# VectorE's two half steps of a pair declared independent of each other, with an empty instruction between direct neighbours

## The chip, the cores and the metric

The kernel runs on one core of one Trainium2 chip. The metric is the device time of one execution in microseconds (us). Engines are named as in the profile: PE is TensorE, PEld its weight loads, DVE is VectorE, ACT is ScalarE, POOL is GpSimd, SP is SyncE.

## The reference

For each of four batches of 6080 tokens with 256 channels a channel attention is computed, and its output goes, token by token, through a feed-forward layer with a rational function in the middle:

```python
def _attn_ref(q, k, v, tau):                     # q, k, v: (4, 6080, 256)
    qn = q / (np.linalg.norm(q, axis=1, keepdims=True) + 1e-06)
    kn = k / (np.linalg.norm(k, axis=1, keepdims=True) + 1e-06)
    s = kn.transpose(0, 2, 1) @ qn / tau
    a = softmax of s over its last axis           # 256 x 256 for each batch
    return v @ a

def _moe_ref(x, w_in, w_out, a, b):              # x: (24320, 256), w_in: (256, 2048), w_out: (2048, 256)
    h = x @ w_in
    h2 = h * h
    h3 = h2 * h
    P = a[0] + a[1] * h + a[2] * h2 + a[3] * h3
    Q = 1.0 + np.abs(b[0]) * np.abs(h) + np.abs(b[1]) * h2
    g = P / (Q + 1e-06)
    return g @ w_out
```

## The kernel before

**Tiling.** The 24320 tokens are cut into 48 groups of 512 (the last of each batch has 448). The 2048 columns of the hidden layer are cut into 8 pairs of two blocks of 128. `pair(m, ...)` is one such pair for one group, so there are 384 of them. The softmax matrix of a batch is multiplied into `w_in` once for each batch (`fuse`), so a pair needs only one product of the values `vhi`, `vlo` with the fused weights `w`.

**A pair on its engines.** The product lands in `hx`, a PSUM tile of two banks, one bank for each block of the pair (tags `hA` and `hB`, index x = 0 and 1 below). There are three such tiles, named hx_176 to hx_178 in listings. PE fills each bank with six matmuls (`mm1`). Then ACT computes `uu` and `d` from hx, and from d the reciprocal `r` (two more steps); DVE turns hx into the numerator ("num", hx<-uu,fast,hx, both banks at once), then writes the high part of the quotient ("quot", gh<-hx,fast,r). What is left is done bank by bank in `tail(x)`: POOL multiplies the denominator by gh ("again", d<-d,gh), DVE subtracts that from the numerator ("rest", hx<-hx,fast,d) and multiplies by r ("last", gl<-hx,r), which is the low part. PE adds gh and gl times `w_out` into `acc` (`out_hi`, `out_lo`). "last" of a bank is the last reader of that bank of hx: after it, PE may fill the bank for a later pair.

**The order.** All steps are put into a list with planned costs and due times (`LAG`, `TIME`), and `Planner.order()` turns it into one fixed program order for each engine. The engine objects are wrapped by `InOrder`, which keeps each engine's instructions in that order. What an instruction waits for is not written by hand: the framework finds dependencies by tile, and it sees the two banks of one hx tile as one tile. `apart` tells it that two instructions on different banks of one hx tile don't depend on each other, but before the change only when they run on different engines (`other is not eng`). So on DVE, "rest" of x = 1 waits for whatever DVE did last on bank 0 of the same tile, and "last" of x = 0 waits for the last step on bank 1 if that stands ahead of it. An instruction can hold a limited number of waits itself; others stand ahead of it on the engine's queue as instructions that only wait (EVENT_SEMAPHORE in the profile).

The kernel has a quick and a general body and picks one at run time by the coefficients. The quick body is the one that runs here. Nearly all instructions are recorded at line 79, since `InOrder` issues them all; tiles tell them apart.

Of the kernel before, what the change touches and what calls it, by code (L numbers as in the profile page):

```python
# [125 lines left out]
def flat(bufs):  # L126
    return [x for b in bufs for x in (b.both if isinstance(b, Pair) else [b])]
# [165 lines left out]
def tile_channel_attention_rational_ffn(  # L293
# [36 lines left out]
    FRONT = 10  # L330

    half = [None]
    seen = {}

    def apart(eng, ins):


        if half[0] is None:
            return
        slot, bank, rest = half[0]  # L340
        for other, old, used in seen.get((slot, 1 - bank), ()):
            if other is not eng and not used & rest:
                tc.declare_no_dep(ins.ins, old.ins, reason="the two use different banks of one tile")
        mine = seen.setdefault((slot, bank), [])
        mine.append((eng, ins, rest))
        del mine[:-40]

    pe = InOrder(tc, nc.tensor, apart)
    dve = InOrder(tc, nc.vector, apart)
    act = InOrder(tc, nc.scalar, apart)  # L350
    pool = InOrder(tc, nc.gpsimd)
    sp = InOrder(tc, nc.sync)
# [15 lines left out]
    def buf(tag, shape, dtype=F32, name=None):  # L368


        def view(slot):
            sizes = dict(zip("abc", shape[1:]))
            t = homes[tag][slot]
            if t.dtype != dtype:
                t = t.bitcast(dtype)
            t = t[:, : math.prod(shape[1:])]
            names = " ".join(sizes)
            return t.rearrange(f"p ({names}) -> p {names}", **sizes) if len(sizes) > 1 else t

        homes.setdefault(tag, 0)  # L380
        homes[tag] = max(homes[tag], math.prod(shape[1:]))
        return Buf(tag, view)
# [75 lines left out]
    def body(quick):  # L458
        lag, when = (LAG, TIME) if quick else (GENERAL_LAG, GENERAL_TIME)
        plan = planner(when)  # L460
        II, T0 = when["pair"], when["start"]
        def step(eng, cost, key, fn, reads=(), writes=(), port=False, rank=None):
            new = [b for b in flat(writes) if b.tag is not None and not b.writers]
            used = {id(b): b for b in (*flat(reads), *flat(writes))}.values()
            own = [b for b in used if b.tag in ("hA", "hB")]
            rest = [b for b in used if b.tag not in ("hA", "hB")]

            def run():
                for b in new:
                    b.tile = b.view(b.slot)  # L470
                at = {(b.slot, b.tag == "hB") for b in own}
                if len(at) == 1:
                    half[0] = *at.pop(), {(b.tag, b.slot) if b.tag else id(b) for b in rest}
                fn()
                half[0] = None

            plan.add(eng, cost, key, run, reads, writes, port, rank)
# [4 lines left out]
        def piece(side, m, at, c):  # L482
# [71 lines left out]
            else:  # L554
                dst, ok = None, w_out_ok[m]
                where = slice(2 * m, 2 * m + 2)
                whi, wlo = (x[:, where].rearrange("p f e -> p (f e)") for x in (w_out_hi, w_out_lo))
            step("SP", 1.45, at, load, (), [raw])
            step("ACT", 0.67, c, rescale, [raw], [kept])
            one, two = (0.45, 0.7) if port else (0.62, 0.7)  # L560
            step("DVE", one, c, low_bits, [kept], [work], port)
            step("DVE", two, c + 0.1, high_bits, [kept, work], [work], port)
            step("DVE", one, c + 0.2, power, [work], [work], port)
# [278 lines left out]
        def pair(m, at, vparts, w, acc):  # L842
# [3 lines left out]
            s = n / 512  # L846
            (vhi, vlo), (whi, wlo) = vparts, w
            hx = banks()
            d, r = buf("d", [P, 2, GT]), buf("r", [P, 2, GT])
            y = buf("uu", [P, 2, GT], F32, "uu")  # L850

            def c(b):
                return b[:, :, :n]

            def due(name):
                x = lag[name]
                return at + (x[p] if isinstance(x, tuple) else x)

            def mm1(i):
                idx = 0  # L860
                for e in range(NC2):
                    for a, x in ((whi, vhi), (whi, vlo), (wlo, vhi)):
                        pe.matmul(
                            hx[:, i, :n], a[:, e, i * P : (i + 1) * P], x[:, e, :n],
                            start=(idx == 0), stop=(idx == 3 * NC2 - 1),
                        )
                        idx += 1

            for i in range(2):
                fn = lambda i=i: mm1(i)  # L870
# [8 lines left out]
                                start=(first and i == parts[0] and a is w[0]), stop=(last and i == 1 and a is w[-1]),  # L879
                            )  # L880

            def put(eng, per, fixed, name, fn, reads, writes, rank=None, later=0.0):
                step(eng, per * s + fixed, due(name) + later, fn, reads, writes, False, None if rank is None else at + rank)

            if quick:
                fn = lambda: act.activation(c(d), c(hx), AF.Abs)
                put("ACT", 0.87, 0.16, "abs", fn, [hx], [d], 1.0)
                fn = lambda: act.activation(c(y), c(hx), AF.Square, bias=half2)
                put("ACT", 0.87, 0.25, "zz", fn, [hx], [y], 1.0)
                fn = lambda: act.activation(c(d), c(d), AF.Square, bias=half1)  # L890
                put("ACT", 0.87, 0.22, "shift", fn, [d], [d])
                fn = lambda: dve.scalar_tensor_tensor(c(hx), c(y), kappa, c(hx), op0=ALU.add, op1=ALU.mult)
                put("DVE", 1.06, 0.23, "num", fn, [y, hx], [hx])
                fn = lambda: act.activation(c(r), c(d), AF.Abs_reciprocal_sqrt, bias=eps)
                put("ACT", 0.87, 0.22, "root", fn, [d], [r], 6.0)
                fn = lambda: pool.tensor_scalar(c(d), c(d), ones[:, 0:1], eps, op0=ALU.mult, op1=ALU.add)
                put("POOL", 1.06, 0.1, "one", fn, [d], [d])
                first = c0
            else:
                kk = buf("uu", [P, 2, GT], F32, "kk")  # L900
                fn = lambda: act.activation(c(kk), c(hx), AF.Abs, scale=b1)
                put("ACT", 0.87, 0.25, "kk", fn, [hx], [kk], 1.0)
                fn = lambda: dve.scalar_tensor_tensor(c(d), c(kk), b0, c(hx), op0=ALU.add, op1=ALU.mult)
                put("DVE", 1.06, 0.22, "prod", fn, [kk, hx], [d], 1.0)
                fn = lambda: act.activation(c(d), c(d), AF.Abs)
                put("ACT", 0.87, 0.2, "absd", fn, [d], [d])
                fn = lambda: act.activation(c(y), c(hx), AF.Identity, scale=a3, bias=a2)
                put("ACT", 0.87, 0.33, "slope", fn, [hx], [y], 1.0)
                fn = lambda: dve.tensor_tensor(c(y), c(y), c(hx), op=ALU.mult)
                put("DVE", 1.06, 0.16, "num1", fn, [y, hx], [y])  # L910
                fn = lambda: dve.scalar_tensor_tensor(c(hx), c(y), a1, c(hx), op0=ALU.add, op1=ALU.mult)
                put("DVE", 1.06, 0.23, "num2", fn, [y, hx], [hx])
                fn = lambda: act.activation(c(r), c(d), AF.Abs_reciprocal_sqrt, bias=ONE)
                put("ACT", 0.87, 0.2, "root", fn, [d], [r], 6.0)
                fn = lambda: pool.tensor_scalar(c(d), c(d), ones[:, 0:1], ONE, op0=ALU.mult, op1=ALU.add)
                put("POOL", 1.06, 0.07, "one", fn, [d], [d])
                first = a0
            fn = lambda: act.activation(c(r), c(r), AF.Square)
# [3 lines left out]
            ghi, glo = buf("gh", [P, 2, GT], F32R), buf("gl", [P, 2, GT], F32R)  # L922
            ghi_ok = Buf()
            t_ok, glo_ok = ([Buf() for _ in range(2)] for _ in range(2))
            fn = lambda: dve.scalar_tensor_tensor(c(ghi), c(hx), first, c(r), op0=ALU.add, op1=ALU.mult)
# [11 lines left out]
            def tail(x):  # L937
                h = hx.both[x]
                fn = lambda: pool.tensor_tensor(d[:, x, :n], d[:, x, :n], ghi[:, x, :n].bitcast(F32), op=ALU.mult)
                put("POOL", 1.16, 0.1, "again", fn, [d, ghi, ghi_ok], [t_ok[x]], later=0.1 * x)  # L940
                fn = lambda: dve.scalar_tensor_tensor(
                    hx[:, x, :n], hx[:, x, :n], first, d[:, x, :n], op0=ALU.add, op1=ALU.subtract
                )
                put("DVE", 0.53, 0.22, "rest", fn, [h, d, t_ok[x]], [h], later=0.1 * x)
                fn = lambda: dve.tensor_tensor(glo[:, x, :n], hx[:, x, :n], r[:, x, :n], op=ALU.mult)
                put("DVE", 0.53, 0.14, "last", fn, [h, r, *([glo] if x else [])], [glo_ok[x], *([] if x else [glo])], 10.0, 0.1 * x)

            for x in range(2):
                tail(x)
                out_hi(x)  # L950
                out_lo(x)
# [70 lines left out]
        for G in range(TG):  # L1022
            b, g = divmod(G, NG)
            at = T0 + G * NFP * II
# [57 lines left out]
```

## Time and profile before

| | |
|---|---|
| median of 3 runs | 2476.43 us (2476.23 to 2478.35) |
| the profiled execution, its own time | 2477.43 us |
| its span, first to last instruction | 2475.4 us |
| busy share of the span | PE 96%, DVE 89%, ACT 88%, POOL 72% |
| mean granted TensorE clock | 0.987 |

The profiled execution is 1.0 us above the median, and 2.0 us of its time lie outside the span. Busy shares are averages over parts of the run that differ: the first 200 us load weights and compute the first attention; in three later parts the attention of the next batch is mixed in between pairs; and in between the pairs run with little else.

### The profile page before, as it was taken

What the parts mean: (1) busy time and instruction counts of PE and PEld (TensorE: products, weight loads), DVE (VectorE), ACT (ScalarE), POOL (GpSimd) and SP (SyncE); (2) the same over time, 40 slices, a digit from 0 to 9 for tenths busy, and PEclk for the clock granted to TensorE, in tenths of its full rate; (3) what the DMA queues carried; (4) which work ended last, traced back from release to release, by engine and by line L of the source; (5) the groups of instructions that cost most, each with busy time, mean ns of one, the idle gap of its engine ahead of it and who ended that gap; (6) DMA issues with size and microseconds to landing.
All of it is one profiled execution on the core that took longest, in us unless ns stands there. A gap on an engine that the chain in (4) does not pass through costs nothing.

```text
span 2475.4 us, 30913 instructions
## 1 busy us (share of the span) xinstructions
PE 2375.3 (96%) x10400; PEld 1942.0 (78%) x10400; DVE 2196.5 (89%) x2684; ACT 2169.3 (88%) x2156; POOL 1770.5 (72%) x1353
## 2 busy tenths in 40 slices
PE   5799999999999999999999999999999999999997
PEld 4677777888788877778788888777878777777786
DVE  6879999988978899999987889999997999999996
ACT  3589999978877899999977789999997999999996
POOL 4387777787679877777768986777774777767765
PEclk9799999999999999999999999999999999999999
DMA  8542112252267611211236731112111110100100
GB/s 248 138 113 42 28 18 35 47 131 56 41 147 171 116 24 18 35 18 18 34 69 157 163 58 25 27 18 35 17 18 20 30 19 18 35 18 18 33 9 18
DMA packets 416890, 141.19 MB, mean 57 GB/s; under 512 B 351344, under 2 KB 406064, under 8 KB 416720
## 3 DMA queue, kind: packets, MB, share of 16 engines
q1 hardware_dynamic: 408176, 108.04, 20.2%
q0 software_dynamic: 8544, 31.07, 7.1%
q8 instruction: 84, 1.38, 0.2%
q14 instruction: 86, 0.70, 0.1%
HBM read 83.10 MB, written 24.90 MB: 44 GB/s over the span
## 4 chain that ended last, share of the span: by engine, by line
PE 74%; DVE 12%; issue 5%; ACT 3%; POOL 2%; DMA 2%; SPq 1%; DVEq 0%; POOLq 0%; ACTq 0%
PE hx L79 40%; PE acc L79 34%; DVE hx L79 5%; DVE gl L79 4%; DVE gh L79 2%; POOL d L79 1%; SPq L79 1%; ACT d L79 1%; ACT r L79 1%; DMA kq<-in_q_dram 1%; DVE orow L79 1%; ACT uu L79 1%; DMA d<-in_moe_w_in_dram 1%; ACT L79 0%; DMA r<-in_k_dram 0%
## 5 line engine op out<-in xcount | busy, mean ns | idle before, releaser
L79 POOL TENSOR_TENSOR d<-d,gh 128x512 f32<-128x512 f32 (+1 forms) x768 | 977.9, 1304 | 498.0 <-DVE gh L79 495.2
L79 PE MATMUL hx<-vhi,w 128*128 128x512 f32 (+1 forms) x3072 | 1046.1, 395 | 30.0 <-DVE gl L79 27.6
L79 PEld LDWEIGHTS hx<-vhi,w 128*128 128x128 f32 x3072 | 579.8, 189 | 195.0 <-DVE gl L79 77.0
L79 DVE SCALAR_TENSOR_TENSOR hx<-hx,fast,d 128x512 f32<-128x512 f32 (+1 forms) x768 | 574.7, 748 | 82.3 <-POOL d L79 53.4
L79 PE MATMUL hx<-vlo,w 128*128 128x512 f32 (+1 forms) x1536 | 598.6, 390 | 0.0
L79 DVE TENSOR_TENSOR gl<-hx,r 128x512 fp32r<-128x512 f32 (+1 forms) x768 | 516.9, 681 | 40.3 <-PE acc L79 3.2
L79 POOL TENSOR_SCALAR d<-d,ones,fast 128x1024 f32<-128x1024 f32 (+1 forms) x384 | 470.7, 1226 | 101.0 <-ACT r L79 100.6
L79 ACT ACTIVATE uu<-hx,fast 128x1024 f32<-128x1024 f32 (+1 forms) x384 | 423.1, 1102 | 135.3 <-PE hx L79 122.9
L79 DVE SCALAR_TENSOR_TENSOR hx<-uu,fast,hx 128x1024 f32<-128x1024 f32 (+1 forms) x384 | 487.2, 1269 | 45.3 <-ACT d L79 35.6
L79 DVE SCALAR_TENSOR_TENSOR gh<-hx,fast,r 128x1024 fp32r<-128x1024 f32 (+1 forms) x384 | 485.8, 1265 | 42.1 <-ACT r L79 34.8
L79 PE MATMUL acc<-gh,w_out_hi 128*128 128x512 f32 (+1 forms) x1536 | 476.7, 392 | 3.2 <-DVE gh L79 2.4
L79 PE MATMUL acc<-gl,w_out_hi 128*128 128x512 f32 (+1 forms) x1536 | 473.8, 390 | 4.4 <-DVE gl L79 4.3
L79 PE MATMUL acc<-gh,w_out_lo 128*128 128x512 f32 (+1 forms) x1536 | 470.3, 387 | 0.0
L79 ACT ACTIVATE r<-d,fast 128x1024 f32<-128x1024 f32 (+1 forms) x384 | 439.7, 1145 | 10.9
L79 ACT ACTIVATE d<-d,fast 128x1024 f32<-128x1024 f32 (+1 forms) x384 | 439.4, 1145 | 8.5
L79 ACT ACTIVATE d<-hx 128x1024 f32<-128x1024 f32 (+1 forms) x384 | 386.5, 1007 | 38.2 <-PE hx L79 32.3
L79 ACT ACTIVATE r<-r 128x1024 f32<-128x1024 f32 (+1 forms) x384 | 403.7, 1052 | 9.1
L79 PEld LDWEIGHTS acc<-gh,w_out_hi 128*128 128x128 f32 x1536 | 287.6, 188 | 65.0 <-ACT orow L79 3.3
L79 PEld LDWEIGHTS acc<-gl,w_out_hi 128*128 128x128 f32 x1536 | 287.8, 188 | 62.9 <-DVE gl L79 6.4
L79 PEld LDWEIGHTS acc<-gh,w_out_lo 128*128 128x128 f32 x1536 | 288.6, 188 | 57.8
L79 PEld LDWEIGHTS hx<-vlo,w 128*128 128x128 f32 x1536 | 290.3, 189 | 52.4
L79 PE MATMUL hx<-kq 128*128 128x256 f32 (+1 forms) x592 | 136.7, 385 | 17.8 <-DVE r L79 17.8
(105 smaller groups left out, 1154.8 us busy)
## 6 DMA issues: line engine op xcount, KB each, us to landing
ssq<-sq POOLq DMA_DIRECT2D x54, 512.0 KB, 4.9
out_dram<-orow SPq DMA_DIRECT2D x178, 128.0 KB, 3.2
vst<-in_v_dram SPq DMA_DIRECT2D x176, 128.0 KB, 3.8
kq<-in_k_dram SPq DMA_DIRECT2D x78, 256.0 KB, 4.4
kq<-in_q_dram SPq DMA_DIRECT2D x78, 256.0 KB, 4.8
d<-in_moe_w_in_dram SPq DMA_DIRECT2D x8, 512.0 KB, 6.9
ssq<-sq POOLq DMA_DIRECT2D x6, 448.0 KB, 5.3
r<-in_k_dram SPq DMA_DIRECT2D x10, 256.0 KB, 6.2
```

The lines of the kernel that those rows point to most:

```text
L79: ins = op(*args, **kwargs)
```

## The change

`apart` gets a fourth entry, `lane`, which is (number of the pair, x) for the steps "rest" and "last" on DVE and None for all others. Two DVE instructions of the same pair and of different x are now declared independent as well. Where two such steps are direct neighbours in DVE's order, `run` issues `dve.nop()` between them, since the declaration would otherwise also remove the order between them.

```diff
     def apart(eng, ins):
         if half[0] is None:
             return
-        slot, bank, rest = half[0]
-        for other, old, used in seen.get((slot, 1 - bank), ()):
-            if other is not eng and not used & rest:
+        slot, bank, rest, lane = half[0]
+        for other, old, used, side in seen.get((slot, 1 - bank), ()):
+            beside = lane is not None and side is not None and lane[0] == side[0] and lane[1] != side[1]
+            if beside or (other is not eng and not used & rest):
                 tc.declare_no_dep(ins.ins, old.ins, reason="the two use different banks of one tile")
         mine = seen.setdefault((slot, bank), [])
-        mine.append((eng, ins, rest))
+        mine.append((eng, ins, rest, lane))
...
             def run():
                 for b in new:
                     b.tile = b.view(b.slot)
+                old = recent.get(eng)
+                if lane is not None and old is not None and old[0] == lane[0] and old[1] != lane[1]:
+                    dve.nop()
+                recent[eng] = lane
...
-                put("DVE", 0.53, 0.22, "rest", fn, [h, d, t_ok[x]], [h], later=0.1 * x)
+                put("DVE", 0.53, 0.22, "rest", fn, [h, d, t_ok[x]], [h], later=0.1 * x, lane=(m, x))
...
-                put("DVE", 0.53, 0.14, "last", fn, [h, r, *([glo] if x else [])], [glo_ok[x], *([] if x else [glo])], 10.0, 0.1 * x)
+                put("DVE", 0.53, 0.14, "last", fn, [h, r, *([glo] if x else [])], [glo_ok[x], *([] if x else [glo])], 10.0, 0.1 * x, (m, x))
```

No instruction changes its place: on all five engines the rows of the two built programs stand in the same order. What changes is what DVE's instructions wait for. Below is a piece of the difference on DVE, with waits shown, from the middle of the quick body (it runs at 1021.8 to 1031.4 us in the profiled execution before). DVE_49 is a wait for an earlier instruction of DVE itself, Pool_49, PE_49 and Activation_49 are waits for POOL, PE and ACT; a minus is the program before, a plus is the changed one, and x2 are two equal rows, one behind the other.

```order
 L79 SCALAR_TENSOR_TENSOR hx_177<-hx_177,fast,d_123 128x512 [waits Pool_49]
 L79 TENSOR_TENSOR gl_174<-hx_177,r_129 128x512 [waits DVE_49,PE_49]
-L79 SCALAR_TENSOR_TENSOR hx_177<-hx_177,fast,d_123 128x512 [waits DVE_49,Pool_49]
+L79 SCALAR_TENSOR_TENSOR hx_177<-hx_177,fast,d_123 128x512 [waits Pool_49]
 L79 SCALAR_TENSOR_TENSOR gh_173<-hx_176,fast,r_131 128x1024 [waits PE_49,Activation_49]
 L79 TENSOR_TENSOR gl_174<-hx_177,r_129 128x512 [waits DVE_49,PE_49]
 L79 SCALAR_TENSOR_TENSOR hx_178<-uu_127,fast,hx_178 128x1024 [waits PE_49,Activation_49]
-L79 SCALAR_TENSOR_TENSOR hx_176<-hx_176,fast,d_125 128x512 [waits Pool_49]
-L79 SCALAR_TENSOR_TENSOR hx_176<-hx_176,fast,d_125 128x512 [waits DVE_49,Pool_49]
-L79 TENSOR_TENSOR gl_175<-hx_176,r_131 128x512 [waits DVE_49,PE_49]
-L79 TENSOR_TENSOR gl_175<-hx_176,r_131 128x512 [waits PE_49]
+L79 SCALAR_TENSOR_TENSOR hx_176<-hx_176,fast,d_125 128x512 [waits Pool_49] x2
+L79 TENSOR_TENSOR gl_175<-hx_176,r_131 128x512 [waits DVE_49,PE_49] x2
```

Two kinds of place are seen. In the first pair (hx_177) the order is rest 0, last 0, rest 1, and rest 1 loses its wait for last 0, its direct neighbour. In the second pair (hx_176) the order is rest 0, rest 1, last 0, last 1: rest 1 loses its wait for rest 0, last 0 now waits for rest 0, which stands two places ahead, in place of rest 1, and last 1 gets a wait for rest 1, which stands two places ahead too. Counted over the quick body, 448 DVE instructions lose a wait for their direct neighbour (326 "rest", 122 "last"), none gets such a wait, and 171 that had no wait for DVE get one for an instruction two or more places ahead. The empty instruction has no row: DVE's queue in the quick body holds 1657 instructions that only wait before and 1374 after, and no other kind of instruction is more or less than before.

## Rows read from the trace of the kernel before

**Rows 1.** The page: busy us, share of the span, instructions of each engine.
```profile
PE 2375.3 (96%) x10400; PEld 1942.0 (78%) x10400; DVE 2196.5 (89%) x2684; ACT 2169.3 (88%) x2156; POOL 1770.5 (72%) x1353
```

**Rows 2.** The page: chain that ended last, shares of the span by engine.
```profile
PE 74%; DVE 12%; issue 5%; ACT 3%; POOL 2%; DMA 2%; SPq 1%; DVEq 0%; POOLq 0%; ACTq 0%
```

**Rows 3.** Windows: stretch, its us, busy us and instructions, granted clock, DMA, GB/s.
```profile
0.00:200.00 200.00, 146.85 (x600) 120.67 (x601) 148.62 (x228) 124.36 (x144) 119.62 (x73) 0.90 0.57 159
200.00:450.00 250.00, 247.32 (x1069) 198.78 (x1068) 239.46 (x280) 241.80 (x230) 181.21 (x140) 1.00 0.17 27
450.00:860.00 410.00, 406.07 (x1812) 338.68 (x1811) 343.39 (x425) 326.82 (x331) 328.69 (x254) 1.00 0.50 105
860.00:1250.00 390.00, 385.13 (x1666) 310.05 (x1665) 372.80 (x435) 375.74 (x357) 280.33 (x216) 1.00 0.16 25
1250.00:1450.00 200.00, 197.29 (x897) 167.89 (x897) 157.98 (x209) 146.56 (x160) 162.51 (x127) 0.99 0.61 131
1450.00:1850.00 400.00, 395.37 (x1715) 319.23 (x1714) 382.86 (x447) 386.05 (x367) 288.56 (x224) 1.00 0.16 25
1850.00:1950.00 100.00, 90.98 (x408) 77.00 (x407) 82.18 (x118) 78.88 (x96) 52.59 (x43) 0.95 0.14 21
1950.00:2430.00 480.00, 474.16 (x2091) 382.09 (x2090) 441.24 (x514) 463.02 (x449) 337.44 (x262) 1.00 0.11 21
```

**Rows 4.** Waits of PE, whole span: us in total, times, longest us.
```profile
PE hx L79 <- DVE gl L79: 29.1, 44, 3.4
```

**Rows 5.** Timeline of PE around 1023 us: start us, us, instruction [idle before].
```profile
1022.39 0.39 PE L79 MATMUL hx<-vhi,w 128*128 128x512 f32 x1
1023.36 0.50 PE L79 MATMUL hx<-vhi,w 128*128 128x512 f32 x1 [0.58 <-DVE gl L79]
1023.70 0.40 PE L79 MATMUL hx<-vlo,w 128*128 128x512 f32 x1
```

**Rows 6.** Chain in order of time, stretch 1050 to 1150 us: start us, us, what.
```profile
1051.44 2.72 PE acc L79 x12
```

**Rows 7.** Timeline of DVE around 1025 us: start us, us, instruction [idle before].
```profile
1021.76 0.75 DVE L79 SCALAR_TENSOR_TENSOR hx<-hx,fast,d 128x512 f32<-128x512 f32 x1
1022.62 0.69 DVE L79 TENSOR_TENSOR gl<-hx,r 128x512 fp32r<-128x512 f32 x1
1023.41 0.76 DVE L79 SCALAR_TENSOR_TENSOR hx<-hx,fast,d 128x512 f32<-128x512 f32 x1
1024.08 1.27 DVE L79 SCALAR_TENSOR_TENSOR gh<-hx,fast,r 128x1024 fp32r<-128x1024 f32 x1
1025.27 0.68 DVE L79 TENSOR_TENSOR gl<-hx,r 128x512 fp32r<-128x512 f32 x1
1025.87 1.28 DVE L79 SCALAR_TENSOR_TENSOR hx<-uu,fast,hx 128x1024 f32<-128x1024 f32 x1
1027.06 0.76 DVE L79 SCALAR_TENSOR_TENSOR hx<-hx,fast,d 128x512 f32<-128x512 f32 x1
1028.10 0.76 DVE L79 SCALAR_TENSOR_TENSOR hx<-hx,fast,d 128x512 f32<-128x512 f32 x1 [0.28 <-POOL d L79]
```

**Rows 8.** Groups of DVE by form: busy us, mean ns | idle before, who ended it.
```profile
L79 DVE SCALAR_TENSOR_TENSOR hx<-hx,fast,d 128x512 f32<-128x512 f32 x704 | 530.6, 754 | 72.1 <-POOL d L79 45.0
L79 DVE TENSOR_TENSOR gl<-hx,r 128x512 fp32r<-128x512 f32 x704 | 477.9, 687 | 36.4 <-PE acc L79 2.0 <-DVE hx L79 0.9
```

**Rows 9.** Groups of ACT in the stretches 200:450, 860:1250, 1450:1850, 1950:2430, one row each.
```profile
L79 ACT ACTIVATE uu<-hx,fast 128x1024 f32<-128x1024 f32 x45 | 49.9, 1108 | 3.7 <-PE hx L79 2.0 <-DVE hx L79 1.5
L79 ACT ACTIVATE uu<-hx,fast 128x1024 f32<-128x1024 f32 x69 | 76.7, 1111 | 7.9 <-PE hx L79 4.0 <-DVE hx L79 3.4
L79 ACT ACTIVATE uu<-hx,fast 128x1024 f32<-128x1024 f32 x69 | 76.7, 1111 | 7.8 <-PE hx L79 4.0 <-DVE hx L79 3.3
L79 ACT ACTIVATE uu<-hx,fast 128x1024 f32<-128x1024 f32 x80 | 88.9, 1112 | 10.7 <-PE hx L79 8.7 <-DVE gl L79 0.7 <-DVE hx L79 0.5
```

**Rows 10.** Waits of PE in the stretch 1850:1950: us in total, times, longest us.
```profile
PE hx L79 <- DVE gl L79: 5.6, 3, 3.4
```

More of the change, by code (lines that the diff above doesn't have):

```diff
@@ L332, in tile_channel_attention_rational_ffn @@
     half = [None]
-    seen = {}
+    seen, recent = {}, {}
     def apart(eng, ins):
@@ L461, in body, with step @@
         II, T0 = when["pair"], when["start"]
-        def step(eng, cost, key, fn, reads=(), writes=(), port=False, rank=None):
+        def step(eng, cost, key, fn, reads=(), writes=(), port=False, rank=None, lane=None):
             new = [b for b in flat(writes) if b.tag is not None and not b.writers]
@@ L470, in run @@
                     b.tile = b.view(b.slot)
+                old = recent.get(eng)
+                if lane is not None and old is not None and old[0] == lane[0] and old[1] != lane[1]:
+                    dve.nop()
+                recent[eng] = lane
                 at = {(b.slot, b.tag == "hB") for b in own}
                 if len(at) == 1:
-                    half[0] = *at.pop(), {(b.tag, b.slot) if b.tag else id(b) for b in rest}
+                    half[0] = *at.pop(), {(b.tag, b.slot) if b.tag else id(b) for b in rest}, lane
                 fn()
@@ L880, in mm2, with put @@
                             )
-            def put(eng, per, fixed, name, fn, reads, writes, rank=None, later=0.0):
-                step(eng, per * s + fixed, due(name) + later, fn, reads, writes, False, None if rank is None else at + rank)
+            def put(eng, per, fixed, name, fn, reads, writes, rank=None, later=0.0, lane=None):
+                step(eng, per * s + fixed, due(name) + later, fn, reads, writes, False, None if rank is None else at + rank, lane)
             if quick:
```

## The prediction

> **What bounds the kernel now.** I read the page first: PE is busy 96% of the span, DVE and ACT 89 and 88% [rows 1], and the chain that ended last runs 74% through PE and 12% through DVE, with almost nothing on ACT and POOL [rows 2]. So PE is the bound, and where it waits, it waits for DVE. The waits of PE name the place: 29.1 us in 44 waits of an hx matmul for DVE's gl step [rows 4], which is "last", the last reader of an hx bank.
>
> Those 29.1 us are too few, since a matmul's shown end hides part of a stall. Matmuls that wait for nothing start every 2.72 / 12 = 0.2267 us [rows 6], though each is shown as 0.39 us. In [rows 5] the step from 1022.39 to 1023.36 is 0.97 us, so the stall is 0.97 - 0.23 = 0.74 us where 0.58 are shown, and the next matmul comes 0.34 us later, 0.11 late as well: 0.85 us in all, half as much again as shown.
>
> The windows show where this matters [rows 3]. Four stretches, 1520 us together, are alike: PE, DVE and ACT are all busy over 90%. The others differ. Before 200 us weights are loaded. In 450:860 and 1250:1450 the next attention's matmuls are mixed in, PE is busy 99% and DVE and ACT have 16 to 27% to spare, so nothing that DVE saves can come out there. 1850:1950 is a hand-over in which PE loses 9 us.
>
> In the four stretches the stall of PE is the time less the count of matmuls by 0.2267: 250 - 242.3 = 7.7 us, 390 - 377.7 = 12.3, 400 - 388.8 = 11.2, and for 1950:2430 480 - 474.0 = 6.0, too little since that stretch holds shorter matmuls; at the 3% of the other three (31.2 of 1040 us) it is 14. Together about 45 us.
>
> **What the change removes.** The price of a wait for the direct neighbour is in [rows 7]. 1021.76 + 0.75 = 1022.51, and the next step starts at 1022.62, 0.11 later; 1022.62 + 0.69 = 1023.31, and rest of x = 1 starts at 1023.41, 0.10 later. Where no such wait stands, the next step starts before the end of the one ahead: 1023.41 + 0.76 = 1024.17 against 1024.08, 1024.08 + 1.27 = 1025.35 against 1025.27, 1025.87 + 1.28 = 1027.15 against 1027.06. So the wait costs 0.10 of idle and 0.08 to 0.09 of lost overlap, 0.19 us. The page shows only the idle half: 72.1 - 45.0 = 27.1 us before the long "rest" steps that POOL did not end, which is 27.1 / 0.105 = 258 of 704, and 36.4 - 2.9 = 33.5 us before "last" [rows 8].
>
> 448 such waits go. Some were covered already, as at 1028.10, where "rest" of x = 1 also waits 0.28 us for POOL [rows 7]. Of the 326 at "rest" about 260 to 280 are bare, at 0.19 about 51 us; the 122 at "last" are 23 us at most. I take 70 us of DVE time over the run; spread over 48 groups that is 1.5 us for each. In the even stretches a group takes 45 us (69 uu steps, one a pair, in 390 us, by eight [rows 9]), so DVE gets 3.2% ahead there, 49 us in 1520. Lower bound of this term: only the idle half counts, 448 x 0.10 = 45 us in the run, 30 in the stretches; upper: 448 x 0.19 = 85.
>
> The Trainium skill speaks against this price. In "VectorE: DVE Perf Modes", section "The DRAIN you can't avoid", it says that a semaphore between chained VectorE operations costs nothing extra, eight copies having taken 13.88 us with one after each and with one after the last alone, and its rules for authors are to save operations, not semaphores. By it the term would be 0 and the time 2476. The trace disagrees with 0.19 us a wait.
>
> **What it adds.** The empty instruction is not in the built program, so it costs nothing. The 171 new waits are for an instruction two or more places ahead. What such a wait costs now is in the same rows: gl at 1025.27 waits for rest, two places ahead, and starts 0.08 before gh ends [rows 7]. I take 0; the other end is the full 0.19, 32 us of DVE time, which still leaves 38 of the 70.
>
> **What becomes of DVE's time.** In each stretch three things limit the gain: PE's stalls (45 us), DVE's saving (49), and what ACT has to spare, since its five steps for each pair must keep up as well. ACT's idle time is before uu, where it waits for PE's product, which waited for DVE: 3.7 + 7.9 + 7.8 + 10.7 = 30.1 us [rows 9]; the rest of its time is its own steps and waits for itself. So ACT sets the limit at 30 us, 2.0% of the 1520. POOL is busy 70 to 75% there and no limit; its result for "rest" follows gh by two POOL steps and moves with it. Three engines so close to full never all run without gaps: I take 0.8 of the 30, 24 us. What is late next is ACT, and DVE will wait for r and d there.
>
> Elsewhere: in 1850:1950 PE waits 5.6 us for gl [rows 10], behind a chain through the softmax of which few steps are halves of a pair; I take 3 us for all other stretches, between 0 and 7.
>
> **Sum.** 24 + 3 = 27 us off the profiled execution's 2477.4, which gives 2450.4. That execution is 1.0 us above the median of the runs, so I predict 2450. A measurement of this kernel can tell 0.2%, 5 us, from no change.
>
> **The rivals.**
> - *The next wait takes most of it.* DVE comes to ACT's r and d sooner and waits there, at the places where ACT is close already, so PE's stalls shrink by a third only: 45 / 3 = 15 less what ACT's order loses, 6 to 17 us, about 2466. For it: PE, DVE and ACT are all above 95% in three of the stretches [rows 3], and three hx tiles couple them. Against: DVE's waits in [rows 7] are for itself and POOL, none for ACT.
> - *No change.* The waits that go were covered, by POOL's result or by PE's own order, or a wait costs nothing, as the skill's page has it: 2476. Against: 448 waits at 0.19 and PE's stalls behind the very step that is freed.
> - *ACT is no limit.* PE's product comes sooner, and ACT's waits for itself shrink with a better overlap: all 45 us of stalls go, 2432. For it: nothing in the rows; against: [rows 9].
> - *Slower.* "rest" on bank 1 now runs into the end of "last" or "rest" on bank 0 of the same tile. If such overlapped half steps got longer by more than the 0.19 us gained, DVE would lose: at 0.25 us more each, 448 x 0.06 = 27 us of DVE time, nearly half of it on PE's path, 2489. It decides from 0.19 on. Against: gl overlaps gh today at 0.68 us, and a gl behind a wait takes 0.69 [rows 7].
>
> **How the numbers follow.** The forecast, 18 to 36 us gained (2441 to 2459), has 0.60; the next wait 0.19; ACT no limit 0.06; no change 0.11; slower 0.04. Faster by over 0.2% is 0.60 + 0.19 + 0.06 = 0.85. The range from 2438 to 2470 holds the forecast, nearly all of the next wait and some of the third: 0.8. It leaves out no change and the slower case.
>
> **What would show it.** DVE's wait-only instructions at 1374 in place of 1657. "rest" of x = 1 starting some 0.08 us before the end of the step ahead, as gh does now; the idle time before "rest" that POOL did not end near zero, and that before "last" smaller by about a third. PE's waits for gl from 29 to under 12 us. ACT's idle before uu in the four stretches from 30 to under 10 us; new or longer waits of DVE for ACT's r and d. The prediction is wrong if PE's waits for gl stay (then DVE's advance was lost ahead of gl), if ACT's waits go but PE's stalls come back elsewhere, or if half steps get longer than 0.76 us.

## The result, and the profile after

The changed kernel took 2437.97 us (median of 4 runs, 2434.53 to 2439.77), the kernel before 2477.34 in 4 runs beside it (2476.23 to 2478.35): ratio 0.984, 95% interval 0.9822 to 0.9857. The gain is 39 us where 27 were forecast, and the time lies just under the range given, 2438 to 2470. The profiled execution is the fastest of the four, 2434.53 us with a span of 2432.5, so the two traces differ by 43 us and the medians by 39.

The page of the changed kernel: busy time of each engine, and the shares of the chain that ended last.
```profile
PE 2353.0 (97%) x10400; PEld 1944.4 (80%) x10400; DVE 2169.6 (89%) x2684; ACT 2160.6 (89%) x2156; POOL 1768.7 (73%) x1353
...
PE 77%; ACT 9%; DVE 7%; issue 4%; DMA 2%; SPq 1%; POOL 0%; DVEq 0%; ACTq 0%; POOLq 0%
```
Against [rows 1, 2], DVE's part of the chain fell from 12% to 7%, and ACT's rose from 3% to 9%.

The waits of PE and of DVE, whole span (us, times, longest), changed kernel:
```profile
DVE gh L79 <- ACT r L79: 54.0, 81, 5.0
...
PE hx L79 <- DVE gl L79: 8.8, 9, 3.0
```
PE's wait of [rows 4] fell from 29.1 us in 44 times to 8.8 in 9. DVE's wait for ACT's r grew; the same view of the kernel before has:
```profile
DVE gh L79 <- ACT r L79: 34.8, 38, 5.0
```

The timeline of DVE at the place of [rows 7], changed kernel:
```profile
1003.50 0.75 DVE L79 SCALAR_TENSOR_TENSOR hx<-hx,fast,d 128x512 f32<-128x512 f32 x1
1004.36 0.69 DVE L79 TENSOR_TENSOR gl<-hx,r 128x512 fp32r<-128x512 f32 x1
1004.96 0.75 DVE L79 SCALAR_TENSOR_TENSOR hx<-hx,fast,d 128x512 f32<-128x512 f32 x1
1005.62 1.28 DVE L79 SCALAR_TENSOR_TENSOR gh<-hx,fast,r 128x1024 fp32r<-128x1024 f32 x1
```
"rest" of x = 1, third row, starts at 1004.96, and the step ahead ends at 1004.36 + 0.69 = 1005.05: 0.09 before its end, where it started 0.10 after it. "last" of x = 0, second row, still waits for its direct neighbour (that wait is real, it reads what "rest" wrote) and starts 0.11 late.

The groups of DVE's half steps (busy, mean ns, idle before and who ended it), changed kernel:
```profile
L79 DVE SCALAR_TENSOR_TENSOR hx<-hx,fast,d 128x512 f32<-128x512 f32 x704 | 522.0, 749 | 43.3 <-POOL d L79 43.0
L79 DVE TENSOR_TENSOR gl<-hx,r 128x512 fp32r<-128x512 f32 x704 | 477.1, 684 | 31.1 <-PE acc L79 5.5 <-DVE hx L79 0.9
```
The idle time before "rest" that POOL did not end is 43.3 - 43.0 = 0.3 us, where it was 27.1. Before "last" it is 31.1 - 6.4 = 24.7, where it was 33.5. The steps did not get longer.

Step by step, with the two traces laid side by side (the order on DVE is the same), 352 half steps, 272 "rest" and 80 "last", went from a start 0.10 us after the end of the step ahead to one 0.09 before it: 67 us in all, 0.19 each. In a count of DVE's starts inside the four even stretches of the prediction, "rest" and "last" come 51.0 us sooner after the step ahead, and 16.8 of them are given back ahead of gh and of the numerator step, which need ACT's r and uu.

The windows of the changed kernel, cut at about the same work as [rows 3] from 200 us on (PE, PEld, DVE, ACT, POOL):
```profile
200.00:442.00 242.00, 241.83 (x1056) 196.84 (x1055) 234.89 (x278) 237.44 (x227) 179.64 (x141) 1.00 0.17 26
442.00:847.00 405.00, 403.09 (x1812) 338.20 (x1811) 340.28 (x424) 326.63 (x331) 327.28 (x253) 1.00 0.52 107
847.00:1226.00 379.00, 379.00 (x1662) 310.20 (x1661) 367.56 (x434) 371.79 (x356) 280.28 (x216) 1.00 0.16 25
1226.00:1426.00 200.00, 198.02 (x901) 169.04 (x900) 156.21 (x209) 147.72 (x161) 162.15 (x127) 0.99 0.61 131
1426.00:1816.00 390.00, 389.57 (x1710) 319.26 (x1709) 377.85 (x446) 382.33 (x366) 288.21 (x224) 1.00 0.17 26
1816.00:1916.00 100.00, 92.09 (x413) 78.24 (x412) 81.37 (x120) 80.45 (x97) 52.91 (x44) 0.95 0.13 21
1916.00:2388.00 472.00, 469.53 (x2089) 382.42 (x2089) 434.41 (x513) 461.55 (x450) 336.79 (x262) 1.00 0.11 22
```
By the prediction's count (time less matmuls by 0.2267), PE's stalls in the first three even stretches are 242 - 239.4 = 2.6, 379 - 376.8 = 2.2 and 390 - 387.7 = 2.3: 7.1 us where 31.2 stood.

For a sharper sum I took the time from the uu step of one pair to that of a later one, in both traces, for the pairs inside the four even stretches (34 groups; gains are taken before rounding):

```
pairs         before    after    gain   groups   gain a group
8 to 56        270.9    265.6     5.3      6        0.88
112 to 184     408.1    398.5     9.5      9        1.06
208 to 280     407.3    398.9     8.4      9        0.93
296 to 376     460.7    453.5     7.3     10        0.73
sum           1547.1   1516.6    30.4
```

So the four stretches gave 30.4 us (24 forecast), and the rest of the 39, some 9 us, came from elsewhere (3 forecast).

ACT's uu steps in the four stretches, changed kernel, one row from each:
```profile
L79 ACT ACTIVATE uu<-hx,fast 128x1024 f32<-128x1024 f32 x44 | 48.6, 1104 | 0.7 <-PE hx L79 0.3
L79 ACT ACTIVATE uu<-hx,fast 128x1024 f32<-128x1024 f32 x69 | 76.3, 1106 | 1.2 <-PE hx L79 0.7
L79 ACT ACTIVATE uu<-hx,fast 128x1024 f32<-128x1024 f32 x69 | 76.4, 1108 | 1.5 <-PE hx L79 0.9
L79 ACT ACTIVATE uu<-hx,fast 128x1024 f32<-128x1024 f32 x81 | 89.9, 1110 | 4.5 <-PE hx L79 4.0
```
Their idle time, 30.1 us in [rows 9], is 7.9: 22.2 us less. That is 8 us short of the 30.4 gained. ACT's uu steps are hardly shorter (1104 to 1110 ns where 1108 to 1112 stood), so ACT must have gained in a way that its idle time does not show. The timeline of ACT shows it, at one place of the kernel before, and in the second fence at the same place of the changed one:
```profile
1026.08 1.16 ACT L79 ACTIVATE r<-d,fast 128x1024 f32<-128x1024 f32 x1
1027.79 1.12 ACT L79 ACTIVATE uu<-hx,fast 128x1024 f32<-128x1024 f32 x1 [0.56 <-PE hx L79]
```
```profile
1008.69 1.15 ACT L79 ACTIVATE r<-d,fast 128x1024 f32<-128x1024 f32 x1
1009.75 1.10 ACT L79 ACTIVATE uu<-hx,fast 128x1024 f32<-128x1024 f32 x1
```
Before, uu starts 1.71 us after the step ahead, with 0.56 shown as idle. After, it starts 1.06 us after it, 0.09 before that step ends. The place gained 0.65 us where 0.56 were shown: a late step on ACT loses its overlap too, as one on DVE does. Between the marks of the table, the time from the start of the step ahead to the start of uu, added up, fell from 311.4 to 283.8 us: 27.6 of the 30.4, of which 22.8 are idle time that the profile shows. Some 2.8 came at ACT's other steps, 1.6 of it before d.

### The profile page after: what moved, and what is told of

It reads as the page before. It is cut to its first block, busy times and chain, and to the rows that moved or that the text cites. A ratio compares the mean times of both kernels' runs of the same rounds, so it can differ in the third digit from the quotient of the medians.

```text
span 2432.5 us, 30630 instructions
## 1 busy us (share of the span) xinstructions
PE 2353.0 (97%) x10400; PEld 1944.4 (80%) x10400; DVE 2169.6 (89%) x2684; ACT 2160.6 (89%) x2156; POOL 1768.7 (73%) x1353
## 4 chain that ended last, share of the span: by engine, by line
PE 77%; ACT 9%; DVE 7%; issue 4%; DMA 2%; SPq 1%; POOL 0%; DVEq 0%; ACTq 0%; POOLq 0%
PE hx L79 42%; PE acc L79 35%; ACT d L79 3%; DVE hx L79 3%; ACT r L79 2%; DVE gl L79 2%; ACT uu L79 2%; SPq L79 1%; DVE gh L79 1%; DMA d<-in_moe_w_in_dram 1%; DMA kq<-in_q_dram 0%; ACT orow L79 0%; DVE orow L79 0%; ACT L79 0%; DMA out_dram<-orow 0%
## 5 line engine op out<-in xcount | busy, mean ns | idle before, releaser
L79 PE MATMUL hx<-vhi,w 128*128 128x512 f32 (+1 forms) x3072 | 1034.0, 392 | 10.3 <-DVE gl L79 8.2
L79 PEld LDWEIGHTS hx<-vhi,w 128*128 128x128 f32 x3072 | 579.3, 189 | 150.3 <-DVE gl L79 33.5
L79 DVE SCALAR_TENSOR_TENSOR hx<-hx,fast,d 128x512 f32<-128x512 f32 (+1 forms) x768 | 565.2, 744 | 50.6 <-POOL d L79 50.2
L79 DVE SCALAR_TENSOR_TENSOR hx<-uu,fast,hx 128x1024 f32<-128x1024 f32 (+1 forms) x384 | 486.9, 1268 | 50.5 <-ACT d L79 39.7
```

The costliest lines, as they stand in the source:

```text
L79: ins = op(*args, **kwargs)
```

## The experiments

Every kernel has 4 to 11 runs beside the kernel before, which stood at 2477 to 2478 us each time. "The four stretches" and gains a group are taken as in the table above, from one execution of each kernel, the first three stretches (24 groups) apart from the last (10 groups).

**The change once more.**

> The changed kernel once more, as the base for the three runs with added work. Both theories: 2438 us, within 3 us.

Measured: 2435.34 us (2433.94 to 2436.29), ratio 0.9832 [0.9818, 0.9845]. The four stretches gained 30.8 us; a group differs by 0.01 us from the first execution of the changed kernel. It is the base for the additions below.

**Which engine sets the pace after the change?** Work is added to one engine, two small pieces a group, in pairs 1 and 5. They use operands that are always there and change no result.

```diff
+    spare = const.tile([P, P], F32, name="spare")
...
                 act.activation(c(r), c(r), AF.Square)
+                if quick and p in (1, 5):
+                    act.activation(spare, ones, AF.Copy)          # more_act
...
+                        if quick and idx == 0 and i == 0 and p in (1, 5):
+                            pe.matmul(hx[:, i, :n], a[:, e, i * P : (i + 1) * P], x[:, e, :n], start=True, stop=True)   # more_pe
                         pe.matmul(
...
                     dve.tensor_tensor(glo[:, x, :n], hx[:, x, :n], r[:, x, :n], op=ALU.mult)
+                    if quick and x == 1 and p in (1, 5):
+                        half[0] = None
+                        dve.tensor_scalar_mul(spare, ones, 1.0)    # more_dve
```

> The changed kernel with 96 short ACT copies into a spare tile (two in each group of eight pairs, behind the second square step); they are estimated at 0.2 us each, 0.4 us a group. Theory A, ACT is what limits the 34 groups of the even stretches now: each 0.4 us shows, 12 to 16 us longer than the changed kernel, about 2452. Theory P, PE is the limit and ACT has time to spare: at most 3 us longer, 2441.

Measured: 2439.49 us, 0.9848 [0.9835, 0.9862], 4.2 over same_again. The copy takes 293 ns by the trace; less 0.10 of overlap that is 0.39 us a group. In the first three stretches a group got longer by 0.18, in the last by 0.01.

> The changed kernel with 96 matmuls done twice (the first of a bank, two in each group), 0.227 us each, 0.45 us a group. Theory P, PE is the limit everywhere: 0.45 x 48 = 22 us longer than the changed kernel, about 2460. Theory A: in the even stretches PE has 43.85 - 43.53 = 0.3 us a group to spare, so 0.15 x 34 = 5 us there, and 0.45 x 12 = 5 us where the attention is mixed in, 10 us in all, about 2448.

Measured: 2443.67 us, 0.9867 [0.9852, 0.9882], 8.3 over same_again. Two matmuls a group are 0.45 us (by 0.2267). In the first three stretches a group got longer by 0.17, in the last by 0.01; the other half of the 8.3 us is outside the four stretches, where PE is the fullest engine.

Less than half of either addition shows, so neither engine alone sets the pace after the change: in the first three stretches ACT has some 0.39 - 0.18 = 0.21 us a group to spare, PE 0.45 - 0.17 = 0.28.

> The changed kernel with 96 short DVE steps into a spare tile (two in each group, behind last of x = 1), 0.28 us each of which 0.08 overlap, 0.4 us a group. Theories A and P: DVE has more than 0.4 us a group to spare now, at most 3 us longer, 2441. Theory D, DVE is still what limits the even stretches: 0.4 x 34 = 14 us longer, 2452.

Measured: 2503.71 us, 1.0101 [1.0086, 1.0117], 68 over same_again. It measured something else than it was meant to. All operations on the new tile of more_dve (min/median/max ns, first and last start), and then its timeline of DVE at one of them:
```profile
L79 DVE TENSOR_SCALAR spare<-ones x96: 205/1018/5880, 154.0 to 2482.2; 128x128 f32<-128x128 f32 x96
```
```profile
1027.33 0.68 DVE L79 TENSOR_TENSOR gl<-hx,r 128x512 fp32r<-128x512 f32 x1
1027.92 1.02 DVE L79 TENSOR_SCALAR spare<-ones 128x128 f32<-128x128 f32 x1
1028.86 1.28 DVE L79 SCALAR_TENSOR_TENSOR hx<-uu,fast,hx 128x1024 f32<-128x1024 f32 x1
```
The operation takes 0.2 us at best and 1.02 at the median. POOL's timeline has two steps there from 1027.56 on, 2.56 us together, so the first ends at 1028.84, and the operation ends at 1028.94, right behind it. Of the 96 operations 88 took over 0.3 us, and each of them ended 0.08 to 0.13 us behind the end of a POOL step. So it priced a block by POOL. The same probe on the kernel before did the same:

> The kernel before with the same 96 DVE steps (0.4 us a group). If DVE set the pace of the even stretches before, as the prediction has it: 0.4 x 34 = 14 us longer than before, 2491. Rival, PE's own order set it and DVE's waits were covered: at most 3 us longer, 2479.

Measured: 2550.07 us, 1.0298 [1.0284, 1.0312], 72 over the kernel before. No verdict on DVE from either.

**And before the change?** The same copies on ACT, in the kernel before.

> The kernel before with the same 96 ACT copies (0.4 us a group). ACT idled 0.9 us a group in the even stretches, so if DVE set the pace at most 4 us longer, 2480. If ACT's steps were on the path already: 12 us or more, 2488.

Measured: 2478.27 us, 1.0006 [0.9997, 1.0015]; 0.02 us a group. ACT had room for 0.39 us a group before the change, and for about half of it after.

**Half of the change.** The lane is given only in pairs of even number; 177 of the 448 waits go.

```diff
-                put("DVE", 0.53, 0.22, "rest", fn, [h, d, t_ok[x]], [h], later=0.1 * x, lane=(m, x))
+                put("DVE", 0.53, 0.22, "rest", fn, [h, d, t_ok[x]], [h], later=0.1 * x, lane=None if p % 2 else (m, x))
... ("last" likewise)
```

> The change for the even pairs of a group alone: 177 of the 448 waits go, 40%. If what DVE saves comes out one for one until ACT is full: 177 x 0.17 = 30 us of DVE time, 21 us of it in the even stretches and 3 elsewhere, 24 us faster than before, 2452. If the gain goes by the share of waits: 40% of 39, 16 us faster, 2460.

Measured: 2458.24 us, 0.9923 [0.9909, 0.9936]: 19.8 us off, half of the gain for 40% of the waits. In a group of the first three stretches 3 bare waits go: 0.57 us at 0.19, 0.31 by the idle half alone. The group got shorter by 0.43 us, more than the idle half. So the lost overlap counts.

**The change without the empty instruction.**

```diff
-                    dve.nop()
+                    pass
```

> The change without the empty instruction: the two half steps are independent, and the framework moves DVE's instructions (its order differs from the planned one in some thousand rows, 98 waits of last for a direct neighbour are left where 263 were). If only waits count: DVE saves 165 x 0.19 = 31 us more and the time is that of the changed kernel or a little less, 2430 to 2438. If the planned order counts, since PE takes the banks in that order: slower than the changed kernel, 2445 or more, and perhaps slower than before.

Measured: 2512.27 us, 1.0146 [1.0131, 1.0162], slower than the kernel before. With nothing between the neighbours, DVE's steps are put into another order than the planned one (all other engines keep theirs). A piece from the start of the quick body, as the two programs list it (plus is what stands there without the empty instruction and not in the changed kernel):

```
 L79 SCALAR_TENSOR_TENSOR gh_172<-hx_176,fast,r_129 128x1024 [waits DVE_49,Activation_49]
+L79 SCALAR_TENSOR_TENSOR hx_177<-hx_177,fast,d_124 128x512 [waits DVE_49,Pool_49]
+L79 SCALAR_TENSOR_TENSOR hx_176<-hx_176,fast,d_123 128x512 [waits DVE_49,Pool_49]
+L79 SCALAR_TENSOR_TENSOR hx_178<-uu_127,fast,hx_178 128x1024 [waits PE_49,Activation_49]
+L79 TENSOR_TENSOR gl_174<-hx_177,r_130 128x512 [waits DVE_49]
```
"rest" of a later pair (hx_176) now stands ahead of "last" of the earlier one, and holds DVE until POOL has its result. The group of "rest" in that kernel:
```profile
L79 DVE SCALAR_TENSOR_TENSOR hx<-hx,fast,d 128x512 f32<-128x512 f32 x704 | 524.6, 752 | 138.5 <-POOL d L79 138.3
```
138.3 us of waiting for POOL where the changed kernel has 43.0. Fewer steps wait for their direct neighbour than in the changed kernel (98 of "last" where 263 did), and the time is longer all the same. The empty instruction leaves nothing in the program and is still worth 74 us here (2512.3 against 2438.0), by the order that it keeps.

**DVE's pace, with a probe that POOL does not block.** A reduction in place of the operation of more_dve, in the kernel before and in the changed one.

```diff
-                        dve.tensor_scalar_mul(spare, ones, 1.0)
+                        dve.tensor_reduce(spare[:, 0:1], ones, axis=AX.X, op=ALU.min)
```

> The kernel before with 96 reductions of one 128x128 tile on DVE (two a group), of a form that ran undisturbed by POOL in no run yet, estimated at 0.2 to 0.3 us each, 0.4 to 0.6 us a group. If DVE sets the pace before the change (the price of 0.19 us a removed wait rests on that), the 34 groups of the even stretches get longer by nearly all of it: 14 to 20 us, 2491 to 2498. If DVE has slack there and only the place of its waits matters, under 5 us.

Measured: 2487.32 us, 1.0048 [1.0035, 1.0062], 10.1 over the kernel before. The new operations of that kernel, and then its timeline of DVE at one of them:
```profile
L79 DVE TENSOR_REDUCE spare<-ones x96: 260/275/280, 154.9 to 2462.3; 128x1 f32<-128x128 f32 x96
```
```profile
1022.10 0.68 DVE L79 TENSOR_TENSOR gl<-hx,r 128x512 fp32r<-128x512 f32 x1
1022.69 0.28 DVE L79 TENSOR_REDUCE spare<-ones 128x1 f32<-128x128 f32 x1
1022.89 1.28 DVE L79 SCALAR_TENSOR_TENSOR hx<-uu,fast,hx 128x1024 f32<-128x1024 f32 x1
```
One takes 1022.89 - 1022.69 = 0.20 us of DVE, 0.40 a group. In the first three stretches a group got longer by 0.32, four fifths of it; in the last by 0.17. The 14 us expected did not come: some 2 us of the shortfall are the fifth that the first three stretches absorb, and some 2 are slack that DVE has in the last one already.

> The changed kernel with the same 96 reductions. Theory: in 200 to 1850 us ACT and PE now set the pace together and DVE has some 0.4 us a group to spare (1.44 us of waits went, 1.05 came out), so a group there gets longer by at most 0.2 us; in 1950 to 2430, where added work of ACT or of PE cost nothing, DVE still sets the pace and a group gets longer by 0.4 to 0.6. Sum 4 to 10 us over the changed kernel, 2440 to 2446. Rival (DVE still sets the pace everywhere, and the waits were worth 1.05 a group and no more): 14 to 20 us, 2450 to 2456.

Measured: 2439.81 us, 0.9848 [0.9834, 0.9861], 4.5 over same_again: 0.16 a group in the first three stretches, 0.16 in the last. DVE went from four fifths to two fifths of a full price where the change gained most; it has 0.24 us a group to spare there now, about as much as ACT and PE. The expectation for the last stretch, the full price, was wrong, before and after the change alike.

**ACT relieved.** A step of uu that stands directly ahead of the step for d of the same pair is moved behind it. On ACT 198 of 883 waits for the direct neighbour go.

```diff
-        return plan.order()
+        return swapped(plan.order())
+
+    def swapped(steps):
+        mine = [s for s in steps if s.eng == "ACT"]
+        for one, two in zip(mine, mine[1:]):
+            if one.name and two.name and one.name[0] == "zz" and two.name == ("abs", one.name[1]):
+                steps.remove(one)
+                steps.insert(steps.index(two) + 1, one)
+        return steps
```
(`name` is the step's name and pair; "zz" writes uu, "abs" writes d.)

> The changed kernel with ACT's step for uu moved behind the step for d of the same pair, where the two are direct neighbours. On ACT 198 of 883 waits for the direct neighbour go, at 0.13 us some 26 us of ACT time, 0.5 us a group. If ACT is one of the limits that the change ran into, the even stretches of 200 to 1850 us gain up to the 0.2 to 0.3 us a group that PE has to spare: 5 to 8 us, 2427 to 2430. Rival: uu comes a step later, DVE waits for it at the numerator step and gives the gain back: 2435 or more.

Measured: 2427.96 us (2426.41 to 2431.59), 0.9802 [0.9789, 0.9815], the fastest kernel of the study, 7.4 below same_again; 6.7 of it in the four stretches, 0.20 a group. The chain of that kernel by engine:
```profile
PE 84%; DVE 7%; ACT 3%; issue 3%; DMA 2%; POOL 1%; SPq 0%; DVEq 0%; ACTq 0%; POOLq 0%
```
ACT's part is back from 9% to 3%. So ACT was one of the limits that the change ran into.

**The change outside the four stretches alone.**

```diff
+    MIXED = (0, *range(7, 14), 23, 24, 25, 35, 36)
-                put("DVE", 0.53, 0.22, "rest", fn, [h, d, t_ok[x]], [h], later=0.1 * x, lane=(m, x))
+                put("DVE", 0.53, 0.22, "rest", fn, [h, d, t_ok[x]], [h], later=0.1 * x, lane=(m, x) if m // 8 in MIXED else None)
... ("last" likewise)
```

> The change only in the 14 groups that lie in the head and in the stretches where the next attention is mixed in (0, 7 to 13, 23 to 25, 35, 36); 116 of the 448 waits go. The prediction gave 3 us, between 0 and 7, to all that lies outside the four even stretches: 2474, inside what can be told from no change. The traces of before and after, taken pair by pair, give 8 us there: 2469. If the gain outside comes only from pairs that arrive earlier out of the even stretches, it is near 0 here.

(The groups listed are 13; the 14 of the expectation is a miscount.)

Measured: 2470.91 us (2467.77 to 2475.28), 0.9976 [0.9967, 0.9985]: 6.3 us, between 3.7 and 8.2, off the kernel before; the four stretches moved by 0.7. So most of the gain outside arises there and is not carried in from the stretches. Pair by pair in its trace, 3.1 us of it lie in pairs 56 to 112 (450:860), 1.8 in pairs 184 to 208 (1250:1450), 0.7 in pairs 280 to 296 and 0.4 in the head. In the traces of before and after, what lies outside the four stretches gained 12.4 us (the changed kernel's execution is 3.4 below the median of its runs): 5.4 in pairs 56 to 112, 1.3 in 184 to 208, 1.6 in 280 to 296, 2.4 in the head and 1.7 behind pair 376.

Two windows of the kernel before that [rows 3] averages in 450:860:
```profile
600.00:650.00 50.00, 49.56 (x215) 39.76 (x214) 47.53 (x57) 48.45 (x47) 35.89 (x28) 1.00 0.14 22
650.00:720.00 70.00, 67.53 (x316) 58.79 (x316) 56.73 (x89) 52.75 (x70) 45.98 (x38) 0.98 0.40 87
```
In the first, DVE is busy 95% and ACT 97%, as in an even stretch, but its pairs (80 to 88) gained 0.3 us alone. In the second, DVE is busy 81% and ACT 75%, and its pairs (88 to 96) gained the most, 2.5 us: there PE loses 2.5 of 70 us, and 2.0 of that are two waits for gl by the view of PE's waits. In all of pairs 56 to 112, 63 of PE's 1713 matmuls start over 0.05 us later behind the one ahead than is usual for its size, 13.2 us together; after the change 42 do, 8.2 us together.

## Why the prediction was off

**Right: the place and the mechanism.** "rest" of x = 1 starts before the end of the step ahead, the idle time before "rest" that POOL did not end is gone (0.3 us), that before "last" fell by 26% (about a third was forecast), PE's waits for gl fell to 8.8 (under 12 forecast), ACT's idle before uu to 7.9 (under 10 forecast), and DVE waits longer for ACT's r (54.0 where 34.8 stood). DVE's term came out too: 67 us at 352 bare waits where 70 were taken, and 51.0 in the stretches where 49 were. That a waiting step carries more waits is not what makes it late: gh at 1024.08 in [rows 7] waits for PE and for ACT, two waits as well, and starts 0.09 before the end of the step ahead.

**Right: the price of a wait, 0.19 us.** half_of_it took away 3 bare waits a group and gained 0.43 us. By before_dve_sum an added microsecond of DVE costs four fifths of one in these stretches; if one taken away gives back as much, 0.57 by 0.8 is 0.46, and the idle half alone would have given 0.25. The Trainium skill's sentence in "VectorE: DVE Perf Modes", section "The DRAIN you can't avoid", that a semaphore between chained operations costs nothing extra (measured there on eight copies), does not hold for this kernel: the two runs say 20 and 39 us.

**The step that failed: "So ACT sets the limit at 30 us".** ACT does become a limit (before_more_act costs nothing, more_act 0.18 a group, and act_turned gains 0.20), but the limit was mis-sized. The prediction priced a late step on DVE with its lost overlap, and on ACT by its idle time alone. Counted from the start times in the trace of before, 90 of the 268 uu steps in the four stretches start late, by 31.0 us in all, and the others 0.10 before the end of the step ahead. A late step that stops being late gives back that 0.10 too: 31.0 + 90 by 0.096 = 39.7 us. The idle half of it came out as forecast, 22.8 us where 0.8 by 30 is 24. What the sum left out is the overlap that came back before uu, 27.6 - 22.8 = 4.8, and the 2.8 at ACT's other steps, which the prediction put at nothing as "its own steps and waits for itself": together 30.4 (42 uu steps are still late after). With 39.7 in place of 30, the factor 0.8 gives 32.

**The second term off: "I take 3 us for all other stretches".** It was some 9. The step behind it was "so nothing that DVE saves can come out there", of 450:860 and 1250:1450, from PE at 99% and from what DVE and ACT have to spare on average. Pairs 56 to 112 gave 5.4 us, the largest part of it where DVE is busy 81%: a share of busy time does not say that nobody waits, and PE's late starts there, 13.2 us before and 8.2 after, do not show in its 99%. mixed_alone gained 6.3 us with the change in these parts only. How the remaining 2 to 3 us split between the head, the last pairs and chance is open: the gain up to the uu step of the first pairs differs by about 1 us between two executions of the changed kernel.

With the two terms as measured, 30.4 + 9 = 39 us; the forecast had 24 + 3.

**The rivals.** *The next wait takes most of it:* DVE does wait more for ACT (the place in [rows 7] has no such wait, but the whole span had 38 already), and a third of what it saved goes back there (16.8 of 51.0), and yet a group gained 0.97 us in the first three stretches, near PE's floor: the chain of the changed kernel in order of time has the same piece one group apart.
```profile
1067.96 2.75 PE hx L79 x12
...
1111.84 2.72 PE hx L79 x12
```
That is 43.88 us, where 192 matmuls by 0.2267 are 43.5. *ACT is no limit* (2432, chance 0.06) came closer in its number than the forecast: PE's stalls in the first three stretches did go from 31.2 to 7.1. But its ground was wrong, since ACT is a limit: with ACT relieved, 6.7 us more came. *No change* and *slower* are out: half steps take 749 and 684 ns, no longer than in [rows 8].

**Still open.** In the last stretch, 1916:2388, added work on ACT costs nothing, before and after, on PE nothing after (before was not tried), and on DVE 0.17 of 0.40 us a group before and 0.16 after, although the change gained 0.73 a group there. No engine alone sets the pace; what does was not tried.

## What to carry to other kernels

Price a wait for the direct neighbour by the start-to-start time, on every engine that it reaches: the idle time that a view shows is what is left after the overlap is already lost (0.10 of 0.19 us on DVE, 0.56 of 0.65 on ACT at one place). When several engines are over 90% busy, an added piece of work of known length on each of them, before and after, tells what each has to spare better than its busy share does. An engine that has time to spare on average still makes others wait at single places (5.4 us came out of a stretch where DVE is 84% busy); count the late starts before calling a stretch's gain nothing.

## What the runs showed of the hardware

A DVE operation of 0.2 us (tensor_scalar, 128x128 from SBUF to SBUF) took 1.02 us at the median and up to 5.9 beside POOL's steps; 88 of 96 took over 0.3 us, and each of these ended 0.08 to 0.13 after the end of a POOL step. A reduction of the same tile took 0.26 to 0.28 us in all 96 places. The Trainium skill, "SBUF — State Buffer", section "Who interferes with whom", has it that tensor_scalar in a two-port mode and GpSimd lock each other out for a whole instruction, and that tensor_reduce never contends on trn2; both agree with these rows, though no row names the mode that the tensor_scalar ran in.
